# One matmul fewer per tile in k'^T x, and the gate's logits moved into the k product

## The chip, the cores and the metric

The kernel runs on one core of one Trainium2 chip. The metric is the device time of one execution in microseconds (us), as the median of several runs. A core has a matmul engine (PE, with its weight loads shown apart as PEld), a vector engine (DVE), a scalar engine (ACT), GpSimd (POOL) and SP, which here only issues DMAs. Each runs its own queue in order; they wait for each other by semaphores. PE writes its results to PSUM, eight banks of 512 fp32 columns on 128 partitions; DVE and ACT read them from there.

## The reference

With x of 2048 x 576, 32 heads of 18 columns and S = 2048:

```python
g = sigmoid((x * gate_w).sum(-1, keepdims=True))
q, k, v = split(x @ wqkv)                     # 32 heads each
phi = lambda t: where(t > 0, t + 1, exp(t)) + 1e-6
kv  = einsum("bhsd,bhse->bhde", phi(k), v);  z = phi(k).sum over s
o   = (phi(q) @ kv) / (phi(q) . z + 1e-6)
a   = o @ wo
b   = Re(DFT_seq(DFT_hidden(x)))              # by real and imaginary matrices
out = g * a + (1 - g) * b
```

## The kernel before, in words

All matmuls take fp32 numbers as a high part, rounded to the type fp32r, and a low part, what is left. A product is three passes: high x high, high x low, low x high. Making the parts ("a split") costs one ACT copy (`hi_of`, L167) and one DVE subtraction (`lo_of`, L177; `lo_later` queues it until the next `tick()`, L182). D = 576 columns are handled as two halves of HALF = 288. A contraction over 576 rows is five chunks: four of 128 rows with three passes, and a rest of 64, doubled to 128, with two: 14 matmuls (`steps`, L263).

The stages that the change touches, in order:

*The k product* (21.1 to 65.6 us, after a start in which the first four tiles are worked chunk by chunk, L484 to L525). For each of the 16 tiles of 128 rows of x, `k_half(i, h, xs)` (L441) runs 14 matmuls for each half h into a bank, and `k_feature` (L446) calls `feature` (L332): ACT does Relu (L334) on the bank and Exp (L335), DVE combines both (L336) into `acc`. After the second half, `k_split` (L451) splits the feature into `pk`: ACT a copy (L167), DVE L453. It is held back until after the next tile's second half. In a turn of the loop (L551) the program issues: first half; its feature; `split_next` for the tile two ahead; `left_part`, one fifth of the making of a factor for the later Fourier products (two additions, two additions, two ACT copies, a long subtraction, another one); second half; its feature; the split of the tile before.

*k'^T x* (L628). For each chunk c of x's columns, four steps of four tiles run `ps[h] += x_tile^T pk[h]`: two banks `ps[0]`, `ps[1]`, three passes (two in the fifth chunk), two halves, so six (four) matmuls of 288 columns a tile (L637). Steps are numbered 0 to 19 through all chunks; the text calls them so. Around each step x's next tiles are loaded (`xg_load`, SP's queue) into four slots and split (`xg_next`; the tile split in step s is used in step s + 2, its low part is issued after the matmuls of step s + 1). After the second step of a chunk come the kv products of the chunk before (`kv_step`, L619 and L622, 252 and 126 columns), weights of the next stages are loaded and split in between, and at a chunk's end the sum is split into `gt`: two ACT copies of 288 columns (L678) and two DVE subtractions, held back (L679).

*The q product* (`q_tile`, L684) from about 126 us: 14 matmuls for each half and the same `feature`. The weights' second half is 290 columns wide here (QH): its last two columns are `gate_w`, so that column 288 of the bank holds the gate's logit. ACT takes Exp of it (L693), DVE adds one (L695) and takes the reciprocal (L696): the sigmoid, in column i of `gate`, one tile at a time. It is used from `L1124` on and in the Fourier stages behind.

What sets the order: SP's queue is written out by hand for the whole kernel, ACT's and DVE's from `pace()` (L483) to the end, so these three issue in program order. PE's order, until the Fourier stages (L1188), is laid out by a planner at build time: it may put q's matmuls or the kv products between the steps of k'^T x. Waits between engines are put in by the framework from what is read and written.

In the Fourier stage, `Hidden.run` (L906), lines 950 to 957 read one bank, `bx`, with both engines:

```python
if p < NP - 2:
    hi_of(fs(0, 0), bx)
else:
    nc.scalar.activation(t(0), bx, AF.Copy)
add(t(4), bx, t(5))
```

Of the kernel before, what the change touches and what calls it, by code (L numbers as in the profile page):

```python
# [8 lines left out]
F = mybir.dt.float32  # L9
R = mybir.dt.float32r  # L10
# [4 lines left out]
P = 128  # L15
# [56 lines left out]
CONST_AT = Y_AT + 2 * D * 4  # L72
XS = 10 * P * 4
WH, WL = 5 * HALF * 4, 4 * HALF * 4
QH = HALF, HALF + 2


LAY_Q = dict(xs=(-256, 4864, 9984, 43776), hi=(15104, 20864), lo=(26688, 31296))


PRODUCTS = {1: (4, 0), 6: (2, 4), 2: (6, 1), 5: (1, 3), 7: (0, 5), 3: (3, 2), 4: (5, 6)}
# [44 lines left out]
def kernel(  # L126
# [36 lines left out]
    def bank():  # L163
        return psum.tile([P, 512], F, tag="bank", name="bank")
# [34 lines left out]
    def half(h):  # L199
        return slice(h * HALF, (h + 1) * HALF)  # L200
# [80 lines left out]
    class Wide:  # L281
# [6 lines left out]
        def load(self, h, pieces=(KC,), queues=None, also=lambda k: None):  # L288

            n = self.widths[h]  # L290
            cols = slice(h * HALF, h * HALF + n)
            hi = at(self.start + self.lay["hi"][h], [P, 5, n], R, "wd")
            los, c = [], 0
            for k in pieces:
                o = self.start + self.lay["lo"][h] + c * n * 4
                los.append((c, at(o, [P, k, n], R, "wd"), at(o, [P, k, n], F, "wraw")))
                c += k
            rest = at(rest_ring.next(), [P, n], F, "wraw")
            self.got[h] = hi, los, rest
            queues = queues or [nc.sync] * (len(pieces) + 1)  # L300
            for i, (c, _, raw) in enumerate(los):
                also(i)
                queues[i].dma_start(out=raw, in_=self.src[:, c:c + raw.shape[1], cols])
            also(len(los))
            queues[-1].dma_start(out=rest, in_=self.src[:, KC, cols])
# [26 lines left out]
    def feature(dst, ps):  # L332
        e = at(es.next(), [P, HALF], F, "e")
        nc.scalar.activation(e, ps, AF.Relu, scale=-1.0)  # L334
        nc.scalar.activation(e, e, AF.Exp, scale=-1.0)  # L335
        nc.vector.scalar_tensor_tensor(dst, ps, 0.0, e, op0=ALU.max, op1=ALU.add)  # L336
# [97 lines left out]
    K_AT = T_AT + NT * XD  # L434
    pk = [at(T_AT + s * XD, [P, 2, D], R, "pk") for s in range(NT)]
    x_at(LAY_Q)
    wkt = Wide(wk, dict(hi=(0, WH), lo=(2 * WH, 2 * WH + WL)), K_AT)

    done = []

    def k_half(i, h, xs):  # L441
        ps = bank()[:, :HALF]
        run(ps, steps(xs, lambda j: wkt.row(h, j)))
        k_feature(i, h, ps)

    def k_feature(i, h, ps):  # L446
        feature(acc[i][:, half(h)], ps)
        if h == 1:
            pending.append(lambda: k_split(i))

# [4 lines left out]

    C_AT = K_AT + 20736
    first, cuts = [], ((0, 1), (1, 1), (2, 2), (4, 1))
    ab = [slice(k * FT // 2 * P, (k + 1) * FT // 2 * P) for k in range(2)]  # L460

# [20 lines left out]
        load_next()  # L482
    pace()  # L483
    for h in range(2):  # L484
        ps = [bank()[:, :HALF] for _ in range(FT)]
        parts = wkt.split(h, KC)
        for c, (raw, hi, lo) in enumerate(first):
            passes = [(hi, c), (lo, c), (hi, 5 + c)][:3 if c < KC else 2]
            tiles = [range(FT)] * len(passes)
            if h == 0 and c == 0:  # L490
                a, b = ab
                nc.vector.tensor_copy(out=hi[:, a], in_=raw[:, a])
                lo_of(lo[:, a], raw[:, a], hi[:, a])
                next(parts)
                done.append(hi_of(hi[:, b], raw[:, b]))
                lo_of(lo[:, b], raw[:, b], hi[:, b])
                two = range(FT // 2), range(FT // 2, FT)
# [75 lines left out]
    tick()  # L573


    wqt = Wide(wq, LAY_Q, widths=QH)
    wq_splits = (s for h in (1, 0) for s in wqt.split(h, 2, lo_later))
    zacc = at(K_AT + 2 * XD, [P, D], F, "zacc")
    zs = at(K_AT + 3 * XD, [P, 2, D], R, "zs")
# [45 lines left out]
    wvt[0], wv_split = load_pair(wv_ring.next(), wv[:, 0])  # L625
    wo_split = []
    step = 0
    for c in range(5):  # L628
        ps = [bank(), bank()]
        passes = FULL if c < KC else FULL[:2]  # L630
        for q in range(NCU):
            t = xg_split.pop(0)
            for k in range(CU):
                s = q * CU + k
                for n, (a, b) in enumerate(passes):
                    for h in range(2):
                        nc.tensor.matmul(ps[h][:, :HALF], t[:, a, k], pk[s][:, b, half(h)],  # L637
                                         start=(s == 0 and n == 0),
                                         stop=(s == NT - 1 and n == len(passes) - 1))
            tick()  # L640
            xg_load()
            if step == NT - 1:
# [31 lines left out]
                next(wq_splits, None)  # L674
            step += 1
        gt = gts[c] = at(gt_ring.next(), [P, 2, D], R, "gt")
        for h in range(2):
            hi_of(gt[:, 0, half(h)], ps[h][:, :HALF])  # L678
            lo_later(gt[:, 1, half(h)], ps[h][:, :HALF], gt[:, 0, half(h)])  # L679
        left_part()  # L680
    tick()


    def q_tile(i):  # L684
        xs = split.pop(0)
        if i == 0:
            split_next()
        for h in range(2):
            ps = bank()[:, :QH[h]]
            run(ps, steps(xs, lambda j: wqt.row(h, j)))  # L690
            g = gate[:, i:i + 1]
            if h:
                done.append(nc.scalar.activation(g, ps[:, HALF:HALF + 1], AF.Exp, scale=-1.0))  # L693
            feature(acc[i][:, half(h)], ps[:, :HALF])
        nc.vector.tensor_scalar(g, g, 1.0, None, op0=ALU.add)  # L695
        nc.vector.reciprocal(out=g, in_=g)  # L696
        load_next()
        if i:
            split_next()
# [109 lines left out]
        f()  # L809
    kv_step(4)  # L810
    q_tile(1)
    build_kv()
    q_tile(2)
    next(norms)
# [393 lines left out]
def _layouts(inputs):  # L1208
# [27 lines left out]
    def right(w):  # L1236
# [17 lines left out]
        "wk": _rows(wqkv[:, D:2 * D]),  # L1254
        "wq": _rows(np.concatenate([wqkv[:, :D], gw, gw], axis=1)),
        "wv": _rows(wqkv[:, 2 * D:]),
        "wo": inputs["A_wo"],
        "xq": left(x.T),
# [27 lines left out]
```

## Time and profile before

| | |
|---|---|
| median of 3 runs | 732.7 us (732.0 to 732.88) |
| profiled execution, first to last instruction (span) | 730.4 us; its own device time isn't listed |
| PE busy | 724.2 us |
| DVE, ACT busy | 601.0 us, 335.6 us |
| TensorE clock granted | 1.000 |

The profile shows one execution. Each engine's instructions are listed with start, length, and in square brackets the idle time ahead of them with the instruction that ended it. "L637" is line 637 of the kernel. Groups carry a count, busy time, mean length in ns and the idle time before. The chain is followed back from the last instruction to what released each; its rows are start, length, what. Lengths of DVE and ACT rows overlap a little at their ends (the next instruction of the queue may start some 0.08 us before a row's end), so the distance between starts is what a queue pays.

### The profile page before, as it was taken

To read this page: it belongs to the slowest core of one execution; us is meant where nothing else is said; L and a number is where in the kernel's file an instruction comes from. 1 tells how busy PE (TensorE), PEld (TensorE's weight loads), DVE (VectorE), ACT (ScalarE), POOL (GpSimd) and SP (SyncE) were. 2 spreads that over 40 slices of the span, in tenths; PEclk is the share of its full clock that TensorE was granted. 3 is DMA by queue.
4 is the path that set the end of the run, shared out by engine and by line. 5 is a ranking of instruction groups with operands and counts; after the bars stand their busy time and mean duration, and the time that the engine had idled before them with its cause. 6 is when DMAs were issued, how large, how long until landed. Compare 5 with 4: busy or idle time off the path is not lost.

```text
span 730.4 us, 13876 instructions
## 1 busy us (share of the span) xinstructions
PE 724.2 (99%) x5444; PEld 722.4 (99%) x5444; DVE 601.0 (82%) x995; ACT 335.6 (46%) x522; POOL 57.0 (8%) x98
## 2 busy tenths in 40 slices
PE   8999999999999999999999999999999999999998
PEld 8999999999999999999999999999999999999997
DVE  5689866779999948989899989767889988788884
ACT  6898435678644444453344334323535332232231
POOL 1011200051032110000000000000000000000000
PEclk9999999999999999999999999999999999999999
DMA  7286787677477999644475666889964544544440
GB/s 254 84 275 217 265 296 234 226 215 224 155 221 298 362 312 383 211 153 135 165 240 177 228 233 202 296 279 395 374 219 130 171 145 135 156 149 148 152 152 33
DMA packets 54356, 158.82 MB, mean 217 GB/s; under 512 B 6420, under 2 KB 11092, under 8 KB 53268
## 3 DMA queue, kind: packets, MB, share of 16 engines
q1 hardware_dynamic: 45044, 118.90, 48.7%
q0 software_dynamic: 8960, 38.65, 14.6%
q8 instruction: 43, 0.70, 0.4%
q10 hardware_dynamic: 288, 0.39, 0.2%
q14 instruction: 21, 0.17, 0.1%
HBM read 115.05 MB, written 41.39 MB: 214 GB/s over the span
## 4 chain that ended last, share of the span: by engine, by line
PE 96%; DMA 2%; DVE 1%; ACT 0%; issue 0%; SPq 0%; DVEq 0%
PE bank L1058 48%; PE bank L197 23%; PE bank L903 14%; PE bank L637 7%; PE bank L512 2%; PE bank L738 1%; DMA wraw<-in_wk_dram 1%; DMA wf<-wm 1%; DMA craw<-in_xg_dram 1%; PE bank L619 0%; DVE row L1074 0%; ACT xb L167 0%; DVE ys L187 0%; PE bank L622 0%; ACT wd L167 0%
## 5 line engine op out<-in xcount | busy, mean ns | idle before, releaser
L1058 PE MATMUL bank<-fh,c 128*128 128x288 f32 x1792 | 357.5, 295 | 0.0
L1058 PEld LDWEIGHTS bank<-fh,c 128*128 128x128 f32 x1792 | 287.5, 188 | 0.0
L1058 PE MATMUL bank<-fl,c 128*128 128x288 f32 x896 | 264.2, 295 | 0.0
L167 ACT ACTIVATE c<-craw 128x1792 fp32r<-128x1792 f32 (+1 forms) x84 | 121.4, 1447 | 187.1 <-DVE craw L187 166.3
L1058 PEld LDWEIGHTS bank<-fl,c 128*128 128x128 f32 x896 | 168.9, 189 | 0.0
L177 DVE TENSOR_TENSOR c<-craw,c 128x1792 fp32r<-128x1792 f32 (+4 forms) x86 | 142.0, 1653 | 5.9 <-ACT c L167 5.7
L187 DVE TENSOR_TENSOR craw<-craw 128x256 f32<-128x256 f32 (+1 forms) x192 | 98.3, 512 | 25.2 <-DMA craw<-in_ci_dram 12.7
L197 PE MATMUL bank<-wd,xs 128*128 128x288 f32 (+1 forms) x784 | 106.3, 296 | 0.4 <-ACT wd L167 0.4
L197 PEld LDWEIGHTS bank<-wd,xs 128*128 128x128 f32 x784 | 104.7, 188 | 0.6 <-ACT wd L167 0.6
L903 PE MATMUL bank<-wf,xf 128*128 128x288 f32 x588 | 92.1, 297 | 0.2 <-DMA wf<-wm 0.2
L903 PEld LDWEIGHTS bank<-wf,xf 128*128 128x128 f32 x588 | 84.0, 189 | 0.4 <-issue 0.4
L197 PE MATMUL bank<-mw,qs 128*128 128x288 f32 x448 | 63.2, 297 | 0.0
L637 PE MATMUL bank<-pk,c 128*128 128x288 f32 x448 | 61.1, 296 | 0.1
L637 PEld LDWEIGHTS bank<-pk,c 128*128 128x128 f32 x448 | 59.9, 189 | 0.3 <-DVE c L177 0.3
L197 PEld LDWEIGHTS bank<-mw,qs 128*128 128x128 f32 x448 | 59.9, 188 | 0.2 <-DVE qs L177 0.2
L187 DVE TENSOR_TENSOR ys<-bank,ys 128x288 f32<-128x288 f32 x63 | 28.8, 457 | 16.1 <-PE bank L1058 12.4
L336 DVE SCALAR_TENSOR_TENSOR acc<-bank,e 128x288 f32<-128x288 f32 x64 | 28.3, 454 | 15.2 <-ACT e L335 13.7
L177 DVE TENSOR_TENSOR fl<-fl,fh 128x864 fp32r<-128x864 f32 (+1 forms) x32 | 34.6, 1093 | 7.1 <-ACT fh L167 5.8
L167 ACT ACTIVATE fh<-fl 128x864 fp32r<-128x864 f32 (+1 forms) x32 | 29.8, 950 | 16.2 <-DVE fl L187 16.2
L903 PE MATMUL bank<-wf,xr 96*128 96x288 f32 x112 | 33.3, 298 | 0.0
L1123 ACT ACTIVATE acc<-bank,gate 128x288 f32<-128x288 f32 x32 | 16.0, 500 | 35.1 <-PE bank L197 34.8
L187 DVE TENSOR_TENSOR ys<-ys,bank 128x288 f32<-128x288 f32 x47 | 21.2, 450 | 12.6 <-PE bank L1058 12.0
(107 smaller groups left out, 665.9 us busy)
## 6 DMA issues: line engine op xcount, KB each, us to landing
xf<-xm SPq DMA_DIRECT2D x42, 512.0 KB, 7.9
craw<-in_cr_dram SPq DMA_DIRECT2D x32, 512.0 KB, 4.1
craw<-in_ci_dram SPq DMA_DIRECT2D x32, 512.0 KB, 3.5
xraw<-in_xa_dram SPq DMA_DIRECT2D x28, 320.0 KB, 4.3
xm<-xb POOLq DMA_DIRECT2D x8, 1024.0 KB, 5.9
wf<-wm SPq DMA_DIRECT2D x14, 576.0 KB, 5.4
xr<-xr SPq DMA_DIRECT2D x14, 448.0 KB, 8.0
xm<-xb POOLq DMA_DIRECT2D x8, 768.0 KB, 5.9
```

Source lines behind the costliest of these rows:

```text
L167: return nc.scalar.activation(dst, src, AF.Copy, bias=bias)
L177: nc.vector.tensor_tensor(out=dst, in0=src, in1=hi, op=ALU.subtract)
L187: nc.vector.tensor_tensor(out=dst, in0=a, in1=b, op=op)
L197: nc.tensor.matmul(ps, a, b, start=(n == 0), stop=(n == len(pairs) - 1))
L336: nc.vector.scalar_tensor_tensor(dst, ps, 0.0, e, op0=ALU.max, op1=ALU.add)
L512: nc.tensor.matmul(ps[i], x[:, i * P:(i + 1) * P], wkt.row(h, j), start=(c == 0 and n == (0 if h or i < 2 else 2)), stop=(c == KC and n == 1))
L637: nc.tensor.matmul(ps[h][:, :HALF], t[:, a, k], pk[s][:, b, half(h)], start=(s == 0 and n == 0), stop=(s == NT - 1 and n == len(passes) - 1))
L738: nc.tensor.transpose(banks[c // KC][:, (c % KC) * P:(c % KC + 1) * P], a, ident)
L903: nc.tensor.matmul(ps, a, b, start=(start and n == 0), stop=(n == len(ops) - 1), skip_group_check=True)
L1058: nc.tensor.matmul(ps[q], c[x][:, l, k], factors[p](y, f), start=(p == 0 and i == 0), stop=(p == NP - 1 and i == 2))
L1123: done.append(nc.scalar.activation(acc[i][:, half(h)], ps[:, :HALF], AF.Copy, scale=gate[:, i:i + 1]))
```

## The change

Three edits. **k'^T x** takes five matmuls for six in a tile: the bank `ps[0]` now holds 512 columns, x's high part times columns 0 to 255 of pk's high part and, beside them, of its low part, in one instruction; `ps[1]` takes columns 256 to 575, 320 wide. At a chunk's end the two halves of `ps[0]` are added: ACT copies one to SBUF, DVE adds the other to it (`raw`), and both parts are split, the 320-column one at once, the other's low part held back. **PE's order** within this loop is the program's. **The gate's logits** come from the k product: `gate_w` stands behind k's weights for q's, DVE copies column 288 of the second half's bank into `gate` ahead of `feature`, and the sigmoid of all 16 columns is computed once, between q tiles 1 and 2. Layouts move by up to 128 bytes to hold the wider weights.

```diff
-QH = HALF, HALF + 2
+KH = HALF, HALF + 2
+CW = 256, D - 256
...
-    wkt = Wide(wk, dict(hi=(0, WH), lo=(2 * WH, 2 * WH + WL)), K_AT)
+    wkt = Wide(wk, dict(hi=(0, WH), lo=(2 * WH + 64, 2 * WH + WL + 64)), K_AT, KH)
...
     def k_half(i, h, xs):
-        ps = bank()[:, :HALF]
+        ps = bank()[:, :KH[h]]
...
     def k_feature(i, h, ps):
-        feature(acc[i][:, half(h)], ps)
+        if h:
+            nc.vector.tensor_copy(out=gate[:, i:i + 1], in_=ps[:, HALF:HALF + 1])
+        feature(acc[i][:, half(h)], ps[:, :HALF])
...
-    wqt = Wide(wq, LAY_Q, widths=QH)
+    wqt = Wide(wq, LAY_Q)
...
+    in_order = tc.manual_schedule(engines={mybir.EngineType.PE})
+    in_order.__enter__()
     for c in range(5):
-        ps = [bank(), bank()]
-        passes = FULL if c < KC else FULL[:2]
+        ps = [bank(), bank()[:, :CW[1]]]
...
-                for n, (a, b) in enumerate(passes):
-                    for h in range(2):
-                        nc.tensor.matmul(ps[h][:, :HALF], t[:, a, k], pk[s][:, b, half(h)],
-                                         start=(s == 0 and n == 0),
-                                         stop=(s == NT - 1 and n == len(passes) - 1))
+                one, last = dict(start=s == 0, stop=False), s == NT - 1
+                if c < KC:
+                    nc.tensor.matmul(ps[1], t[:, 1, k], pk[s][:, 0, CW[0]:], **one)
+                nc.tensor.matmul(ps[0].rearrange("p (b n) -> p b n", b=2), t[:, 0, k],
+                                 pk[s][:, :, :CW[0]], start=s == 0, stop=last and c == KC)
+                if c < KC:
+                    nc.tensor.matmul(ps[0][:, :CW[0]], t[:, 1, k], pk[s][:, 0, :CW[0]],
+                                     start=False, stop=last)
+                    one["start"] = False
+                nc.tensor.matmul(ps[1], t[:, 0, k], pk[s][:, 0, CW[0]:], **one)
+                nc.tensor.matmul(ps[1], t[:, 0, k], pk[s][:, 1, CW[0]:], start=False, stop=last)
...
-        for h in range(2):
-            hi_of(gt[:, 0, half(h)], ps[h][:, :HALF])
-            lo_later(gt[:, 1, half(h)], ps[h][:, :HALF], gt[:, 0, half(h)])
+        t = at(es.next(), [P, CW[0]], F, "e")
+        raw = at(K_AT + c % 2 * XD + D * 4, [P, CW[0]], F, "graw")
+        nc.scalar.activation(t, ps[0][:, CW[0]:], AF.Copy)
+        add(raw, ps[0][:, :CW[0]], t)
+        hi_of(gt[:, 0, CW[0]:], ps[1])
+        lo_of(gt[:, 1, CW[0]:], ps[1], gt[:, 0, CW[0]:])
+        hi_of(gt[:, 0, :CW[0]], raw)
+        lo_later(gt[:, 1, :CW[0]], raw, gt[:, 0, :CW[0]])
         left_part()
+    in_order.__exit__(None, None, None)
...
-            ps = bank()[:, :QH[h]]
+            ps = bank()[:, :HALF]
             run(ps, steps(xs, lambda j: wqt.row(h, j)))
-            g = gate[:, i:i + 1]
-            if h:
-                done.append(nc.scalar.activation(g, ps[:, HALF:HALF + 1], AF.Exp, scale=-1.0))
-            feature(acc[i][:, half(h)], ps[:, :HALF])
-        nc.vector.tensor_scalar(g, g, 1.0, None, op0=ALU.add)
-        nc.vector.reciprocal(out=g, in_=g)
+            feature(acc[i][:, half(h)], ps)
...
     q_tile(1)
+    done.append(nc.scalar.activation(gate, gate, AF.Exp, scale=-1.0))
+    nc.vector.tensor_scalar(gate, gate, 1.0, None, op0=ALU.add)
+    nc.vector.reciprocal(out=gate, in_=gate)
     build_kv()
```

More of the change, by code (lines that the diff above doesn't have):

```diff
@@ L74 @@
 WH, WL = 5 * HALF * 4, 4 * HALF * 4
-QH = HALF, HALF + 2
-LAY_Q = dict(xs=(-256, 4864, 9984, 43776), hi=(15104, 20864), lo=(26688, 31296))
+KH = HALF, HALF + 2
+CW = 256, D - 256
+LAY_Q = dict(xs=(-256, 4864, 9984, 43776), hi=(15104, 20864), lo=(26624, 31232))
 PRODUCTS = {1: (4, 0), 6: (2, 4), 2: (6, 1), 5: (1, 3), 7: (0, 5), 3: (3, 2), 4: (5, 6)}
@@ L293, in load @@
             los, c = [], 0
+            lo, raw = (at(self.start + self.lay["lo"][h], [P, KC, n], d, name)
+                       for d, name in ((R, "wd"), (F, "wraw")))
             for k in pieces:
-                o = self.start + self.lay["lo"][h] + c * n * 4
-                los.append((c, at(o, [P, k, n], R, "wd"), at(o, [P, k, n], F, "wraw")))
+                los.append((c, lo[:, c:c + k], raw[:, c:c + k]))
                 c += k
@@ L454, in k_split @@
                                        op0=ALU.add, op1=ALU.subtract)
-    C_AT = K_AT + 20736
+    C_AT = K_AT + 20864
     first, cuts = [], ((0, 1), (1, 1), (2, 2), (4, 1))
@@ L484 @@
     for h in range(2):
-        ps = [bank()[:, :HALF] for _ in range(FT)]
+        ps = [bank()[:, :KH[h]] for _ in range(FT)]
         parts = wkt.split(h, KC)
@@ L1253, in _layouts @@
         "xg": twice.reshape(NT, P, 5, P).transpose(2, 1, 0, 3),
-        "wk": _rows(wqkv[:, D:2 * D]),
-        "wq": _rows(np.concatenate([wqkv[:, :D], gw, gw], axis=1)),
+        "wk": _rows(np.concatenate([wqkv[:, D:2 * D], gw, gw], axis=1)),
+        "wq": _rows(wqkv[:, :D]),
         "wv": _rows(wqkv[:, 2 * D:]),
```

## The prediction

> **What bounds the kernel now.** I read the page's head first, then engine use by stage, then the chain that ended last, then each queue around the edits.
>
> ```profile
> span 730.4 us, 13876 instructions
> ...
> PE 724.2 (99%) x5444; PEld 722.4 (99%) x5444; DVE 601.0 (82%) x995; ACT 335.6 (46%) x522; POOL 57.0 (8%) x98
> ```
>
> PE is busy for 724.2 of 730.4 us, so any pause that the change puts into PE lengthens the run by its own length. The change touches two stages, the k product (21.1 to 65.6 us) and k'^T x behind it (to 132). The first in the windows view (columns: stretch and length, then PE, PEld, DVE, ACT and POOL busy, clock, DMA):
>
> ```profile
> 21.10:65.60 44.50, 44.50 (x338) 44.50 (x337) 36.65 (x67) 39.91 (x84) 5.19 (x8) 1.00 0.62 208
> ```
>
> In the k product ACT is busy for 39.9 of 44.5 us and DVE for 36.7: both are nearly full and both run in program order, so there PE's lead over them is what has to be watched.
>
> ```profile
> 21.13 44.55 PE bank L197 x336
> ...
> 99.65 12.85 PE bank L637 x96
> ...
> 185.00 0.55 PE bank L738 x5
> ```
>
> From the chain: a 288-column matmul costs 44.55/336 = 132.6 ns in the k product (3.71 us for a tile's 28), 12.85/96 = 133.9 ns in k'^T x, and a 128-column transpose 0.55/5 = 110 ns.
>
> **Part 1: five instructions for six.** For each of the 16 tiles of a chunk of x columns with all three passes the columns stay 6 x 288 = 1728 = 320 + 512 + 256 + 320 + 320; in the fifth chunk 4 x 288 = 512 + 320 + 320. So 4 x 16 + 16 = 80 instructions go and no column does. What is saved is the part of 133.9 ns that doesn't grow with columns. No 512-column matmul is in this trace; the nearest narrower rows are the kv products, where 252 and 126 columns alternate (weight loads of L619, one pair apart):
>
> ```profile
> 85.04 0.19 PEld L619 LDWEIGHTS bank<-gt,plain 128*126 128x126 f32 x1
> ...
> 85.26 0.19 PEld L619 LDWEIGHTS bank<-gt,plain 128*126 128x126 f32 x1
> ```
>
> A pair takes some 0.225 us. The 126-column one can't be much under the transpose's 110 ns, so 252 columns take 115 to 119, and the line through (252, 117 +-2) and (288, 133.9) has a slope of 0.41 to 0.52 ns per column: the fixed part lies between 0 and 15 ns, the saving between 0 and 80 x 15 = 1.2 us. I take the middle, **-0.7 us**. The 256-column matmul stays above the 110 ns floor, so nothing new is exposed.
>
> The Trainium skill, "TensorE: Matmul & The Clock Gate", section "Back-to-back issue gap", gives some 131 ns as the sustained spacing at 512 columns. Here 288 columns already take 133.9, so the trace speaks against it; by it the edit would save some 80 x 134 ns = 10.7 us, the last rival below.
>
> **Part 2: the logits in the k product.** The matmuls of k's second half get 290 columns for 288, those of q's lose the same two: 224 each, nothing in sum. In q this goes (ns min/median/max):
>
> ```profile
> L693 ACT ACTIVATE gate<-bank x16: 152/171/171, 134.9 to 196.9; 128x1 f32<-128x1 f32 x16
> L695 DVE TENSOR_SCALAR gate<-gate x16: 143/145/147, 137.2 to 198.2; 128x1 f32<-128x1 f32 x16
> L696 DVE RECIPROCAL gate<-gate x16: 162/164/167, 137.4 to 198.4; 128x1 f32<-128x1 f32 x16
> ```
>
> That is 2.7 us of ACT and 4.9 of DVE, all beside PE, which has no gap there: worth nothing. The three operations that replace it lie between q tiles and cost nothing either. In the k product DVE gets 16 copies of one column; by these rows some 0.15 us each, 2.4 us in 44.5 of which DVE has 7.9 to spare. Taken as work, nothing.
>
> But the copy reads the bank that ACT's Relu (L334) reads next. What do two engines on one bank do here? Lines 952 to 955 answer: ACT copies bank `bx` to one tile, DVE adds the same bank to another; neither uses what the other writes.
>
> ```profile
> 268.95 0.41 ACT L167 ACTIVATE fh<-bank 128x288 fp32r<-128x288 f32 x1 [2.50 <-PE bank L903]
> 269.40 0.46 DVE L187 TENSOR_TENSOR fl<-bank,fl 128x288 f32<-128x288 f32 x1 [0.85 <-ACT fh L167]
> L187 DVE TENSOR_TENSOR fl<-bank,fl 128x288 f32<-128x288 f32 x8 | 3.6, 455 | 1.7 <-ACT fh L167 1.4 <-ACT fl L954 0.2
> ```
>
> DVE starts 0.04 us after ACT's read ends, and the group row puts its idle time before all of these additions down to the two ACT reads of that bank (L167, and L954 where line 954 makes it). So reads of one bank by two engines are ordered as the program has them, and the Relu of every second half will wait for DVE's copy, which stands in DVE's queue behind that tile's x split and left part. That is a new wait on the fuller engine. (Here both read the same columns; in the change the columns differ, and this is the rival.)
>
> The Trainium skill, "PSUM — Partial Sum Buffer", section "Terms", counts two engines in one bank as a collision, reads against reads included, whichever columns they read; by that rule different columns don't help. The rows above agree where the columns are the same.
>
> What it costs, first at the start of the stage:
>
> ```profile
> 22.76 0.39 ACT L334 ACTIVATE e<-bank 128x288 f32<-128x288 f32 x1
> 22.89 0.76 DVE L453 SCALAR_TENSOR_TENSOR pk<-acc,pk 128x576 fp32r<-128x576 f32 x1 [0.75 <-ACT pk L167]
> ...
> 27.84 0.82 DVE L177 TENSOR_TENSOR xs<-xraw,xs 128x640 fp32r<-128x640 f32 x1 [0.17 <-ACT xs L167]
> ```
>
> Tile 0's Relu waits for its copy, +0.16. Tile 1's copy follows tile 0's pk split on DVE (22.89 + 0.16 + 0.67), so its Relu starts at about 23.9 for 22.76, +1.1; tile 2's again a pk split later, +2.1; tile 3's copy waits for tile 2's whole feature, +2.8. By then the low part of tile 6's x split (27.84 to 28.66) is 2.8 us late. PE wants it at 28.56 (tiles 4 and 5 from 21.13 at 3.71 us), or 0.26 later for the low half, and now has it 0.2 early: PE pauses **2.6 us**. Then it turns into a ring of two in-order queues. Its pieces now, on ACT and on DVE:
>
> ```profile
> 53.28 0.67 ACT L167 ACTIVATE pk<-acc 128x576 fp32r<-128x576 f32 x1
> 53.86 0.39 ACT L334 ACTIVATE e<-bank 128x288 f32<-128x288 f32 x1
> 54.28 0.45 ACT L335 ACTIVATE e<-e 128x288 f32<-128x288 f32 x1
> 54.63 0.72 ACT L167 ACTIVATE xs<-xraw 128x640 fp32r<-128x640 f32 x1
> ```
>
> ```profile
> 39.23 1.22 DVE L177 TENSOR_TENSOR xb<-xb,xb 128x1024 fp32r<-128x1024 f32 x1
> ...
> 41.40 0.45 DVE L336 SCALAR_TENSOR_TENSOR acc<-bank,e 128x288 f32<-128x288 f32 x1
> 41.77 0.82 DVE L177 TENSOR_TENSOR xs<-xraw,xs 128x640 fp32r<-128x640 f32 x1
> 42.50 0.95 DVE L177 TENSOR_TENSOR xb<-xb,xb 128x768 fp32r<-128x768 f32 x1
> ...
> 45.50 0.76 DVE L187 TENSOR_TENSOR xb<-xb 128x256 f32<-128x256 f32 x2
> ```
>
> From copy to copy, by the starts of neighbouring rows (a row's own length less 0.08 where its neighbour isn't shown): copy 0.18, Relu 0.42, Exp 0.35, pk split 0.58, the next half's Relu 0.42, Exp 0.35, x split on ACT 0.75 until DVE may go on, its low part on DVE 0.73, left part 0.67 to 1.14 (the rows of xb; mean about 0.87), and the next copy: 4.65 us, against PE's 3.71. Today it doesn't close, since ACT's Relu asks only for PE. x splits of tiles 6 to 15 make nine turns: 9 x 0.94 = 8.5 us. With the start, **+11.1**; I bound it by 9 and 13.
>
> k'^T x then begins with its queues late: its third step's tile comes some three turns after tile 15's x split, short of x work at the end, about 13.5 us; PE needs it one k tile and two steps later, 3.71 + 2 x 3.2 = 10.1. **+3.4** (2 to 4.5).
>
> **Part 3: the sum of the two banks, in PE's program order.** At the end of each chunk DVE gets an addition and a split ahead of the x split that PE wants in the second step after.
>
> ```profile
> 107.85 0.95 DVE L177 TENSOR_TENSOR xb<-xb,xb 128x768 fp32r<-128x768 f32 x1
> 108.72 0.69 DVE L177 TENSOR_TENSOR c<-craw,c 128x512 fp32r<-128x512 f32 x1
> ...
> 121.49 0.43 DVE L177 TENSOR_TENSOR c<-craw,c 128x256 fp32r<-128x256 f32 x1 [0.66 <-ACT c L167]
> ```
>
> ```profile
> 122.47 0.69 ACT L167 ACTIVATE gt<-bank 128x288 fp32r<-128x288 f32 x2
> 114.89 0.38 SPq L303 DMA_DIRECT2D wraw<-in_wq_dram  x1
> ```
>
> Third chunk (its last two steps of 24 matmuls begin at 99.65, 3.21 us each, so it ends at 106.07): Copy 0.42, addition 0.42, low part 0.48, left part 1.14, then the x split, 0.69 as in 108.72: 109.2, where PE wants it at 99.65 + 3 x 3.21 = 109.3. Cost 0, cover 0.1 us; I take the first two chunks alike. In the fourth, the Copy takes the place of the gt row, 122.47, on ACT; the low part of step 17's tile (121.49 now) moves to 122.47 + 0.42 + 0.42 + 0.48 = 123.8, 2.3 us later, and PE, which now may not put the kv products ahead of step 17, has only q's first 14 matmuls (1.86 us) to fill in. The left part of 107.85 is also 2 to 3 us later; its store holds SP's wq load (114.89), behind which the last x loads queue. Together 0 to 5 us; I take **+2.5**.
>
> **Sum.** 11.1 + 3.4 + 2.5 - 0.7 = +16.3 us. The profiled span is 730.4; the median of the runs is 732.7, 2.3 above it for what lies around the span, and I add to the median: **749.0**, bounds 9 + 2 + 0 - 1.2 = +9.8 (742) and 13 + 4.5 + 5 = +22.5 (755).
>
> **Rivals.**
> - *Reads of different columns aren't ordered* (for: the rows show equal columns only). The copies then fit DVE's idle time and the k product stays as it is. What is left is Part 3: with its wait, 732.7 + 2.5 - 0.7 = 734.5 (733 to 737). Chance 0.10.
> - *The same, and q's matmuls fill the wait*: 732.7 - 0.7 = 732.0 (731 to 733). Against it: only 14 of them are ready. Chance 0.07.
> - *A matmul's spacing doesn't grow with columns above 288*, and the Relu isn't held: 80 x 133.9 ns = -10.7 us, 722. It decides from the first chunk on, if 512 columns pass in under 150 ns. Against it is the step from 117 to 133.9 ns over 36 columns. This is the faster side. Chance 0.03.
>
> **How the numbers follow.** The forecast has 0.80, nearly all within 740 to 756, so that range holds about 8 in 10. A measurement tells some 0.2% (1.5 us) from no change: slower 0.80 + 0.07 of the first rival; same 0.03 of it and 0.05 of the second; faster 0.02 of the second and 0.03: 0.05.
>
> **What would show it.** Right: ACT's Relu (now L334) in the k product idle for DVE's gate copy, about 1 us a tile; 4.6 us between x splits; PE pauses on xs; the first k'^T x matmul some 11 us later. Wrong: Relu idle only for PE there, and the k product ending by 67 us; then this forecast fails as a whole. For Part 1: 20 matmuls of four tiles in 3.16 us would say 14 ns fixed, in 3.21 none. For Part 3: PE's idle time ahead of step 17.

## The result and the profile after

The changed kernel takes 760.8 us (median of 5, 760.0 to 762.4) beside 732.9 us for the kernel before in the same runs (732.0 to 734.0). The ratio is 1.038, with a 95% interval of 1.0368 to 1.0392. It is 27.9 us slower. The forecast was 749.0 with a range of 740 to 756: the direction was right, the size was too small.

The page after, head and use of the engines:

```profile
span 758.9 us, 13692 instructions
...
PE 735.2 (97%) x5364; PEld 723.4 (95%) x5364; DVE 604.1 (80%) x986; ACT 337.8 (45%) x512; POOL 57.0 (8%) x98
```

The 80 matmuls are gone (5444 to 5364), and DVE, ACT and POOL do the same work as before to 1%. The span grew by 28.5 us all the same, so what is new are pauses and slow stretches of PE. The waits of PE after (columns: what waited for what, total us, times, longest):

```profile
PE bank L198 <- ACT xs L168: 4.8, 8, 2.2
PE bank L643 <- DVE c L178: 4.3, 1, 4.3
PE bank L516 <- DVE wd L178: 3.7, 1, 3.7
PE bank L642 <- DVE c L178: 3.7, 5, 1.5
...
PE bank L198 <- ACT kvb L168: 1.2, 1, 1.2
```

They lie in five places: the k product (xs), step 17 of k'^T x (L643), the start (L516), steps 0, 1, 2, 5 and 13 of k'^T x (L642), and once a product of the q stage (kvb). Of these the start and the last have no term in the forecast. To see what each place costs, take the starts of the same PE rows in both timelines:

| start of | before | after | later by | grown since the row above |
|---|---|---|---|---|
| the loop over tiles (tile 4) | 20.96 | 26.05 | 5.1 | 5.1 |
| tile 15 (before: 20.96 + 11 tiles of 3.71) | 61.8 | 78.35 | 16.6 | 11.5 |
| the kv products of chunk 2 | 112.34 | 134.20 | 21.9 | 5.3 |
| the first transpose | 184.84 | 213.97 | 29.1 | 7.2 |
| the end | 730.4 | 758.9 | 28.5 | -0.6 |

**The k product** goes as forecast. The group of the Relus, and two turns of the timeline (start, length, engine, line; idle time ahead in brackets):

```profile
L336 ACT ACTIVATE e<-bank 128x288 f32<-128x288 f32 x64 | 25.7, 402 | 34.4 <-DVE gate L450 22.6 <-PE bank L198 10.2 <-DVE pz L720 0.8
```

```profile
42.40 0.15 DVE L450 COPY gate<-bank 128x1 f32<-128x1 f32 x1
42.59 0.41 ACT L336 ACTIVATE e<-bank 128x288 f32<-128x288 f32 x1 [1.76 <-DVE gate L450]
...
51.93 0.15 DVE L450 COPY gate<-bank 128x1 f32<-128x1 f32 x1
52.12 0.41 ACT L336 ACTIVATE e<-bank 128x288 f32<-128x288 f32 x1 [2.09 <-DVE gate L450]
```

Relu reads columns 0 to 287 of the bank and the copy column 288, and Relu still starts 0.04 us after the copy's end, having stood 1.76 and 2.09 us for it; 22.6 us in all. So reads of different columns are held in order too, by the waits that the framework puts in. Two turns take 9.53 us. PE's rows show the ring: tile 6 waits 2.16 us, and tile 15 comes nine turns later, (78.35 - 35.82) / 9 = 4.73 us each.

```profile
35.82 4.61 PE L198 MATMUL bank<-wd,xs 128*128 128x288 f32 x21 [2.16 <-ACT xs L168]
...
73.40 4.31 PE L198 MATMUL bank<-wd,xs 128*128 128x288 f32 x28 [0.26 <-ACT xs L168]
78.35 4.32 PE L198 MATMUL bank<-wd,xs 128*128 128x288 f32 x28 [0.64 <-ACT xs L168]
84.17 0.41 PE L642 MATMUL bank<-pk,c 128*128 128x320 f32 x1 [1.50 <-DVE c L178]
```

**The start** holds something that the prediction did not see. DVE, then PE:

```profile
9.77 0.46 DVE L178 TENSOR_TENSOR wd<-wraw,wd 128x288 fp32r<-128x288 f32 x1 [4.58 <-DMA wraw<-in_wk_dram]
```

```profile
10.28 7.88 PE L516 MATMUL bank<-wd,xs 128*128 128x288 f32 x46 [3.71 <-DVE wd L178]
```

The low part of the first piece of k's weights waits for a DMA of k's weights. Before, PE's pause at this place was 0.56 us:

```profile
9.20 11.93 PE L512 MATMUL bank<-wd,xs 128*128 128x288 f32 x88 [0.56 <-ACT wd L167]
```
The reason is an edit of `Wide.load` that is not among the three edits listed ahead of the prediction and of which the prediction says nothing: where each piece of the weights had tensors of its own, one tensor for raw and one for low parts, both at the same memory, now spans all pieces of a half.

```diff
+            lo, raw = (at(self.start + self.lay["lo"][h], [P, KC, n], d, name)
+                       for d, name in ((R, "wd"), (F, "wraw")))
             for k in pieces:
-                o = self.start + self.lay["lo"][h] + c * n * 4
-                los.append((c, at(o, [P, k, n], R, "wd"), at(o, [P, k, n], F, "wraw")))
+                los.append((c, lo[:, c:c + k], raw[:, c:c + k]))
```

A low part is written over its own raw numbers through the other tensor. With one pair of tensors for all pieces, the write into piece 0 is treated as if it touched all of raw, and waits until the other pieces have landed.

**The end of a chunk.** Around step 17, ACT and DVE, then PE:

```profile
144.54 0.63 ACT L168 ACTIVATE c<-craw 128x512 fp32r<-128x512 f32 x1 [0.98 <-DMA craw<-in_xg_dram]
145.25 0.68 ACT L168 ACTIVATE plain<-wraw 128x576 fp32r<-128x576 f32 x1
145.84 0.43 ACT L168 ACTIVATE wd<-wraw 128x288 fp32r<-128x288 f32 x1
146.17 0.36 ACT L690 ACTIVATE e<-bank 128x256 f32<-128x256 f32 x1
```

```profile
146.57 0.42 DVE L188 TENSOR_TENSOR graw<-bank,e 128x256 f32<-128x256 f32 x1 [2.22 <-ACT e L690]
147.56 0.49 DVE L178 TENSOR_TENSOR gt<-bank,gt 128x320 fp32r<-128x320 f32 x1 [0.56 <-ACT gt L168]
147.96 0.41 DVE L178 TENSOR_TENSOR c<-craw,c 128x256 fp32r<-128x256 f32 x1
```

```profile
148.48 0.77 PE L643 MATMUL bank<-pk,c 128*128 128x512 f32 x1 [4.26 <-DVE c L178]
```

Read it backwards. PE waits for the low part of step 17's tile (147.96). DVE had nothing to do for 2.22 us before it, but that low part stands in its queue behind the addition `graw`, the addition waits for ACT's Copy of the bank, and the Copy stands in ACT's queue behind the split of c (step 17's own tile, which had to wait 0.98 us for its load), a split of wv and one of wq. The bank itself had its last matmul by 141.7. So an addition that nobody needs soon carries what holds ACT through two in-order queues to PE. Not all of the 4.26 us is the addition's: ACT was through with step 17's tile only at 145.17, so its low part of 0.41 us could not have been there before 145.6, and PE had finished step 16 at 144.2. Some 1.4 us is the late load. All five additions find DVE idle for the Copy:

```profile
L188 DVE TENSOR_TENSOR graw<-bank,e 128x256 f32<-128x256 f32 x5 | 2.1, 422 | 11.4 <-ACT e L690 11.4
```

That is 11.4 us of idle DVE in sum.

**The clock.** The windows view of PE (stretch, length, busy, clock granted, DMA share, GB/s):

```profile
10.28:14.90 4.62, 4.62 (x23) 0.63 0.79 302
35.80:40.40 4.60, 4.53 (x22) 0.69 0.03 9
148.40:153.00 4.60, 4.52 (x15) 0.50 0.05 18
```

Behind these three pauses PE has a lower clock for some 4.6 us: 0.63 at the start (4.62 x 0.37 = 1.7 us lost), 0.69 behind tile 6's wait, 0.50 behind step 17's (2.3 us lost). The first matmul there has a row of 0.77 us. The clock before was 1.00 throughout. So this pause of 4.26 us costs about 6.5.

The five rows of matmuls of a tile, for part 1 of the forecast:

```profile
140.12 0.39 PE L643 MATMUL bank<-pk,c 128*128 128x512 f32 x1
140.35 0.28 PE L646 MATMUL bank<-pk,c 128*128 128x256 f32 x1
140.47 0.30 PE L649 MATMUL bank<-pk,c 128*128 128x320 f32 x1
140.61 0.31 PE L650 MATMUL bank<-pk,c 128*128 128x320 f32 x1
140.75 0.31 PE L642 MATMUL bank<-pk,c 128*128 128x320 f32 x1
140.90 0.39 PE L643 MATMUL bank<-pk,c 128*128 128x512 f32 x1
```

By the distance of the starts, 512 columns take 0.23 us, 256 take 0.12, 320 take 0.14 to 0.15; this tile takes 140.90 - 140.12 = 0.78 us where six of 133.9 ns took 0.803. Single tiles vary by 0.02 us, so a long stretch tells more: in a later kernel (sum last, own memory for raw) the starts of the first 24 tiles of k'^T x run from 65.69 to 83.88 without a pause, 0.791 us a tile, and before 24 tiles took from 65.51 to 84.69, 0.799 each. That is 8 ns for each instruction that went, 0.7 us for 80.

### The profile page after: what moved, and what is told of

It is laid out like the page before. It is cut to its first block, busy times and chain, and to the rows that moved or that the text cites. A ratio compares the mean times of both kernels' runs of the same rounds, so it can differ in the third digit from the quotient of the medians.

```text
span 758.9 us, 13692 instructions
## 1 busy us (share of the span) xinstructions
PE 735.2 (97%) x5364; PEld 723.4 (95%) x5364; DVE 604.1 (80%) x986; ACT 337.8 (45%) x512; POOL 57.0 (8%) x98
## 4 chain that ended last, share of the span: by engine, by line
PE 81%; DVE 7%; ACT 6%; DMA 4%; issue 2%; SPq 0%; DVEq 0%; ACTq 0%
PE bank L1073 44%; PE bank L198 15%; PE bank L918 14%; PE bank L516 2%; ACT e L337 1%; PE bank L643 1%; ACT e L336 1%; ACT pk L168 1%; PE bank L750 1%; DVE c L178 1%; ACT xs L168 1%; DVE xs L178 1%; DVE xb L178 1%; PE bank L649 1%; PE bank L650 1%
## 5 line engine op out<-in xcount | busy, mean ns | idle before, releaser
L198 PE MATMUL bank<-wd,xs 128*128 128x288 f32 (+1 forms) x784 | 112.7, 301 | 6.6 <-ACT xs L168 4.8
L198 PEld LDWEIGHTS bank<-wd,xs 128*128 128x128 f32 x784 | 106.7, 191 | 11.1 <-ACT xs L168 7.1
L338 DVE SCALAR_TENSOR_TENSOR acc<-bank,e 128x288 f32<-128x288 f32 x64 | 28.4, 455 | 28.1 <-ACT e L337 26.5
L336 ACT ACTIVATE e<-bank 128x288 f32<-128x288 f32 x64 | 25.7, 402 | 34.4 <-DVE gate L450 22.6
L168 ACT ACTIVATE fh<-fl 128x864 fp32r<-128x864 f32 (+1 forms) x32 | 29.8, 950 | 16.1 <-DVE fl L188 16.1
L643 PE MATMUL bank<-pk,c 128*128 128x512 f32 x80 | 32.7, 409 | 4.4 <-DVE c L178 4.3
```

Source lines behind the costliest of these rows:

```text
L168: return nc.scalar.activation(dst, src, AF.Copy, bias=bias)
L198: nc.tensor.matmul(ps, a, b, start=(n == 0), stop=(n == len(pairs) - 1))
L643: nc.tensor.matmul(ps[0].rearrange("p (b n) -> p b n", b=2), t[:, 0, k], pk[s][:, :, :CW[0]], start=s == 0, stop=last and c == KC)
```

## The experiments

All run beside the kernel before, whose median was 733.26 us for the first four below, 733.29 for the next four, 733.42 for the three after and 733.07 for the last. The theory is the reading above: four causes (the copy's place, the shared tensors of the weights' pieces, the chunk's end, the clock after pauses). Its rivals are that the clock or the order of PE does it by itself, or that two of the causes are one.

**The copy behind the feature.** The changed kernel with the two lines of `k_feature` exchanged:

```diff
-        if h:
-            nc.vector.tensor_copy(out=gate[:, i:i + 1], in_=ps[:, HALF:HALF + 1])
         feature(acc[i][:, half(h)], ps[:, :HALF])
+        if h:
+            nc.vector.tensor_copy(out=gate[:, i:i + 1], in_=ps[:, HALF:HALF + 1])
```

> The DVE copy of the gate's column stands behind feature() in the program instead of ahead of it. Theory (the Relu of each second half waits for the copy, and two in-order queues close a ring): the Relu's idle time for the gate copy, 22.6 us, goes; the k product's tiles take 3.71 us again; the run loses some 15 us of its 28, to about 746 us. Rival (16 more DVE operations reading PSUM are themselves what fills the stage, wherever they stand): within 2 us of 760.8. The start (first matmul of the loop over tiles at 26.05 us) stays as it is under both.

Measured: 746.9 us (746.5 to 748.2), ratio 1.0184 (1.0169 to 1.0199), 13.9 us less than the changed kernel. The group of Relus lost its wait for the copy altogether, and PE goes from the loop's start to the end of the k product without a pause:

```profile
L336 ACT ACTIVATE e<-bank 128x288 f32<-128x288 f32 x64 | 25.6, 400 | 16.7 <-PE bank L198 12.5 <-PE bank L516 2.6 <-DVE pz L720 0.8
```

The copies are still there, at the same bank. It was their place ahead of Relu, not their work. The start did not stay quite as it was: in this run's profile the loop over tiles begins at 24.73 for 26.05, so some 1.3 us of the lead may be the start's.

**Own tensors for the pieces.** `Wide.load` as before for the halves of 288 columns (the wider half keeps the new form):

```diff
-            lo, raw = (at(self.start + self.lay["lo"][h], [P, KC, n], d, name)
-                       for d, name in ((R, "wd"), (F, "wraw")))
+            if n != HALF:
+                lo, raw = (at(self.start + self.lay["lo"][h], [P, KC, n], d, name)
+                           for d, name in ((R, "wd"), (F, "wraw")))
             for k in pieces:
-                los.append((c, lo[:, c:c + k], raw[:, c:c + k]))
+                if n == HALF:
+                    o = self.start + self.lay["lo"][h] + c * n * 4
+                    los.append((c, at(o, [P, k, n], R, "wd"), at(o, [P, k, n], F, "wraw")))
+                else:
+                    los.append((c, lo[:, c:c + k], raw[:, c:c + k]))
```

> Only Wide.load is changed: the first half's pieces of k's weights are tensors of their own again, with the same 290-column layout in DRAM. Theory (with one tensor for all pieces the first low split waits for the load of the last piece): DVE's wait of 4.58 us for wraw goes, the loop over tiles starts near 21 us for 26.05, and the run takes about 756 us. Rival (rows of 2312 bytes in DRAM load more slowly): the start stays at 26 us and the time within 1 us of 760.8.

Measured: 758.0 us (757.6 to 758.4), ratio 1.0333 (1.0317 to 1.0348), 2 us above the expectation. DVE's low part of the first piece no longer waits:

```profile
4.76 0.45 DVE L178 TENSOR_TENSOR wd<-wraw,wd 128x288 fp32r<-128x288 f32 x1
```

It starts at 4.76 instead of 9.77, and the loop over tiles begins at 21.09 instead of 26.05. At the first transpose the lead is still 5.5 us (208.49 for 213.97), but the run is only 2.8 us shorter: later, PE now waits 1.0 us for a factor's load and 0.8 for a split of the last stage, 0.3 and 0.2 in the changed kernel. The cause at the start is shown; a part of what it costs is hidden by loads that come when they come.

**Both.**

> Both edits together. Theory that the end-of-chunk block and PE's fixed order cost by themselves: 760.8 - 15 - 5 = 741 us, PE idle some 4 us ahead of step 17 of k'^T x with its clock lowered behind it. Rival (that wait was only the k product's lag passed on): it goes with the lag, and the time is 732 us, just under the kernel before.

Measured: 742.6 us (741.5 to 743.9), ratio 1.0123 (1.0108 to 1.0138). With the copy's wait gone, the pieces are worth 746.9 - 742.6 = 4.3 us; with own pieces, the copy's place is worth 758.0 - 742.6 = 15.4. The rest to the kernel before, 9.4 us, lies behind the k product.

**The five matmuls alone**, put into the kernel before (with the chunk's end and PE's order, without the gate's move and without the edit of `Wide.load`; the diff is the part of the change under `for c in range(5)`).

> The kernel before with k'^T x alone changed (five matmuls, the sum of two banks, PE in program order); the gate is as before. Theory: the same time as e3 within 1 us (about 740 us: the wait ahead of step 17 less 0.9 us for 80 instructions), so that the gate's move itself, done rightly, is worth nothing. Rival (the wait is the k product's lag): 732 us.

Measured: 741.6 us (741.1 to 741.7), ratio 1.0107 (1.009 to 1.0124), 8.3 us over the kernel before: nearly all of the 9.4 us that the two repairs leave. This edit, meant to take work from PE, costs 8.3 us by itself. Its waits of PE in k'^T x and the window behind step 17's wait:

```profile
83.07 0.41 PE L639 MATMUL bank<-pk,c 128*128 128x320 f32 x1 [1.66 <-DVE c L178]
...
129.09 0.76 PE L640 MATMUL bank<-pk,c 128*128 128x512 f32 x1 [4.46 <-DVE c L178]
```

```profile
128.00:134.00 6.00, 4.91 (x17) 0.51 0.21 64
```

```profile
L188 DVE TENSOR_TENSOR graw<-bank,e 128x256 f32<-128x256 f32 x5 | 2.1, 425 | 16.1 <-ACT e L687 16.1
```

1.7 ahead of step 5, 0.5 in two small ones, 4.5 ahead of step 17, 4.91 x 0.49 = 2.4 by the clock, less the dropped instructions' 0.7: 8.4, close to the measured 8.3 (the spans of the two profiles lie 9.3 apart). And the chunk's end is as late without any lag from the k product: the additions stand 16.1 us for the Copy. Ahead of step 5 it is the queues alone:

```profile
79.28 0.69 ACT L168 ACTIVATE plain<-wraw 128x576 fp32r<-128x576 f32 x1 [2.67 <-DMA wraw<-in_wv_dram]
79.87 0.37 ACT L687 ACTIVATE e<-bank 128x256 f32<-128x256 f32 x1
80.27 0.42 DVE L188 TENSOR_TENSOR graw<-bank,e 128x256 f32<-128x256 f32 x1 [2.93 <-ACT e L687]
...
82.33 0.68 DVE L178 TENSOR_TENSOR c<-craw,c 128x512 fp32r<-128x512 f32 x1
```

The chunk's last matmul ended at 78.25, but the Copy comes at 79.87, behind a split of wv that stood 2.67 us for its load. Step 5's low part (82.33), whose tile ACT had split at 75.97, stands behind the addition.

**The gate's move alone**, with the copy where the change has it and own tensors for the pieces (k'^T x as before).

> Only the gate's move: the logits come from the k product with DVE's copy ahead of the feature, the sigmoid is computed once; k'^T x and its PE order are those of the kernel before, and the first half's pieces of k's weights are tensors of their own. Theory: the ring between DVE's copy and ACT's Relu alone, 733.3 + 14 = 747 us, with the loop over tiles 11 us longer and k'^T x waiting some 3 us at its start. Rival (part of the 14 us that moving the copy gave back in the changed kernel came from its end-of-chunk block being hit by the lag): 740 to 743.

Measured: 749.9 us (749.2 to 753.7), ratio 1.0232 (1.0201 to 1.0263): +16.6, 3 more than expected (the profile is of the slowest of the four runs, 753.7). Its timeline has tile 6 waiting 2.12 us and tile 15 at 73.21, nine turns of 4.73 us as in the changed kernel; k'^T x then waits in five places, 2.4 us, and the q product 0.5 us for weights and 1.2 us for `kvb`, a wait that every kernel with the gate's move shows (0.8 to 1.5 us) and the five matmuls alone don't. Where tile 15 starts it is 11.4 us behind the kernel before, at the kv products of chunk 2 (127.58) 15.2: 3.8 us is the late begin of k'^T x without the five matmuls. The five matmuls alone are 2.2 us behind at the same place (114.50).

The three effects add up: 8.3 + 16.6 + (2.8 to 4.3) = 27.7 to 29.2, measured 27.9. So neither edit needs the other to do harm.

**PE's order.** Both repairs, without the two `in_order` lines, so that the planner lays out PE's order as before.

> e3 (copy behind the feature, pieces on their own) without PE's fixed program order in k'^T x: the planner at build time may put kv and q matmuls between the steps again. Theory (the wait ahead of step 17 comes from DVE's and ACT's queues, and there is little that PE could do meanwhile): 742 us, within 2 us of e3's 742.6. Rival (the fixed order itself costs the 9 us): 733 to 735.

Measured: 741.2 us (740.1 to 742.1), ratio 1.0103 (1.0083 to 1.0122), 1.4 us less than with the order held, at the edge of what the spread tells. PE now waits 1.9 us for the addition `graw`, 1.5 and 0.5 for c, 0.5 for gt, with the clock lowered behind (0.73 over 4.6 us). The order is not what costs 8 us: the planner cannot move what DVE and ACT do in program order.

**The sum behind what PE needs.** Both repairs, and the chunk's end in another order: the left part and the held-back low parts (`tick`) come ahead of the addition.

```diff
         nc.scalar.activation(t, ps[0][:, CW[0]:], AF.Copy)
-        add(raw, ps[0][:, :CW[0]], t)
         hi_of(gt[:, 0, CW[0]:], ps[1])
+        left_part()
+        tick()
+        add(raw, ps[0][:, :CW[0]], t)
         lo_of(gt[:, 1, CW[0]:], ps[1], gt[:, 0, CW[0]:])
         hi_of(gt[:, 0, :CW[0]], raw)
         lo_later(gt[:, 1, :CW[0]], raw, gt[:, 0, :CW[0]])
-        left_part()
```

> e3 with DVE's queue at a chunk's end in another order: the left part and the held-back x split come first, the addition of the two banks and its split after them; ACT's Copy and the 320-column high part stay where they were. Theory (the block at a chunk's end holds up the x split that PE needs next): PE's waits of 1.7 us ahead of step 5 and 4.2 ahead of step 17 shrink to under 0.5 and under 2 us, the clock isn't lowered any more (2.4 us), in all 735 to 737 us. Rival (the last x tiles arrive late because SP's wq load is late): the wait of 4.2 us shrinks by less than 1.5 us, 739 to 741.

Measured: 735.6 us (734.0 to 736.5), ratio 1.0027 (1.0015 to 1.0038): 7.0 us of the 9.4 are gone by issuing the same instructions in another order. DVE around the end of chunk 3:

```profile
121.99 0.43 DVE L178 TENSOR_TENSOR c<-craw,c 128x256 fp32r<-128x256 f32 x1 [0.77 <-ACT c L168]
122.74 0.76 DVE L178 TENSOR_TENSOR plain<-wraw,plain 128x576 fp32r<-128x576 f32 x1 [0.32 <-ACT plain L168]
123.53 0.46 DVE L178 TENSOR_TENSOR wd<-wraw,wd 64x288 fp32r<-64x288 f32 x1
124.02 0.42 DVE L188 TENSOR_TENSOR graw<-bank,e 128x256 f32<-128x256 f32 x1
```

Step 17's low part (121.99) now stands ahead of the addition (124.02), and the waits ahead of steps 5 and 17 are gone, the lowered clock with them (the windows of this stage show 1.00). So Part 3's cause is the order of a chunk's end. For step 5 that is the place of the addition in DVE's queue. For step 17 the edit moved two things at once, since the left part now comes earlier too: SP's load of wq waits for the left part's store (5.5 us with both repairs), goes out at 115.32 for 119.29, and with it the load of step 17's tile comes earlier. ACT's split of that tile, with both repairs and here:

```profile
125.33 0.63 ACT L168 ACTIVATE c<-craw 128x512 fp32r<-128x512 f32 x1 [0.93 <-DMA craw<-in_xg_dram]
```

```profile
121.33 0.63 ACT L168 ACTIVATE c<-craw 128x512 fp32r<-128x512 f32 x1 [0.90 <-DMA craw<-in_xg_dram]
```

With both repairs PE had finished step 16 at 125.06, so by these rows some 1.3 of its 4.2 us would have stayed with the addition out of the way. No run separates the two.

**raw in memory of its own.** In the changed kernel `raw` lies in the memory of gt's low half, and ACT's copy of the 320 columns waits for the addition (0.55 us at 147.09). Both repairs, and:

```diff
-        raw = at(K_AT + c % 2 * XD + D * 4, [P, CW[0]], F, "graw")
+        raw = at(Y_AT + 3 * 1184, [P, CW[0]], F, "graw")
```

> e3 with raw, the sum of the two banks, in memory of its own instead of in the place of gt's low part. Theory (two tensors that share memory are waited for as wholes): ACT's high part of 320 columns no longer waits for DVE's addition (0.55 us at each chunk's end), the block is about 1 us shorter, PE's waits ahead of steps 5 and 17 are 0.5 to 1 us shorter each: about 740.5 us. Rival (those waits are real ones, for the bank or the engine): the same waits, 742.6 us.

Measured: 740.0 us (739.3 to 740.4), ratio 1.0086 (1.0068 to 1.0104), 2.6 us less than both repairs. The pauses ahead of steps 5 and 17 are 1.0 and 3.4 us for 1.7 and 4.2, and the clock behind the latter 0.70 for 0.50: 0.7 + 0.8, and 4.91 x (0.50 - 0.30) = 1.0, together 2.5.

**Towards a better kernel.** Three kernels with the sum last: with own memory for raw, the same without the held order, and without the held order but with raw's memory shared.

> The five matmuls with the gate's copy behind feature(), own tensors for the pieces, the sum of the halves behind the left part, and raw in memory of its own (kernel e9_sum_last with the memory of e11_own_raw). Theory (the end of each chunk decides, by the one-engine chain from the stopped bank to the first split): with no wait of TensorE above 1.5 us left between 66 and 190 us, the time is that of before less the 0.9 us of the dropped instructions, plus what is left of the waits, 732 to 734.5 us. Rival (the order of TensorE's program, written out for this stage, costs something by itself): 734.5 to 736.5, no better than e9_sum_last, since it leaves the order as it is.

> The kernel of e12_last_own_raw without the region that holds TensorE to the order in which the program is written. Theory (the end of the chunk decides): within 1.5 us of e12_last_own_raw, 731 to 734.5 us. Rival (the written order costs something by itself): 1.5 to 3 us below e12_last_own_raw.

> The kernel of e9_sum_last (raw still in the memory of gt's low half) without the region of TensorE's order. Theory: 734 to 736 us, as e9_sum_last, since the sum lies behind the splits in program order and the shared memory costs 0.55 us of the low half alone. Rival (the shared memory holds back the high half as well): above 736.

Measured: 735.9 us (ratio 1.0036, 1.0024 to 1.0049), 734.9 (1.0015, 1.0006 to 1.0024) and 734.9 (1.0025, 1.0014 to 1.0035). The first came out above its expectation, at its rival's number (the held order costs something), and no better than the sum last alone. Without the held order the same kernel takes 1.0 us less, the intervals just touching, though still above its expected 731 to 734.5; with raw's memory shared the ratios differ by 0.0002 only. So the held order costs 1.4 us at most, by the two repairs. With the addition out of the way, the shared memory costs nothing that can be told. What is left in the first one's waits:

```profile
PE bank L628 <- DVE gt L178: 1.4, 1, 1.4
PE bank L198 <- ACT kvb L168: 1.3, 1, 1.3
```

A last kernel, built on the first of these three, moved the kv products of chunk 3 one step back, those of chunk 4 ahead of the splits of wo, and the sigmoid behind the sums of the kv blocks:

```diff
-            if q == 1 and c:
+            if q == (2 if c == 4 else 1) and c:
                 kv_step(c - 1)
...
-    for f in wo_split:
-        f()
     kv_step(4)
+    for f in wo_split:
+        f()
     q_tile(1)
+    build_kv()
     done.append(nc.scalar.activation(gate, gate, AF.Exp, scale=-1.0))
     nc.vector.tensor_scalar(gate, gate, 1.0, None, op0=ALU.add)
     nc.vector.reciprocal(out=gate, in_=gate)
-    build_kv()
```

> The kernel of e12_last_own_raw with the kv products of chunk 3 one step later (behind step 18's matmuls for step 17's), those of chunk 4 ahead of the splits of wo, and the gate's sigmoid behind the sums of the kv blocks for ahead of them. The waits of TensorE that e12_last_own_raw still shows in this stage are 1.4 us ahead of the kv products of chunk 3 and 1.3 us ahead of a product of the q tiles that needs a bank of the kv blocks. Theory (the new end of a chunk costs what TensorE waits for it and nothing else): both waits go, and the time is 2 to 3 us below e12_last_own_raw's 735.9, 732.9 to 733.9 us, the same as the kernel before within 0.1%. Rival (the kv products are late for a reason that moves with them, VectorE's backlog, so that the wait comes back one step later): no change, 735 to 737 us, 0.3 to 0.4% above the kernel before.

Measured: 736.8 us (735.2 to 737.6), ratio 1.0044 (1.0029 to 1.0058): the rival's number. The wait for gt went, but PE now got to q's first products 1.6 us ahead of their weights, with a clock of 0.68 behind that and a wait of 0.4, and `kvb` still costs 0.8:

```profile
126.35 0.40 PE L198 MATMUL bank<-wd,xs 128*128 128x288 f32 x1 [1.55 <-ACT wd L168]
```

So no kernel here beats the one before. What makes the `kvb` wait in all kernels with the gate's move stays open: the sigmoid's place alone does not explain it.

## Why the prediction was wrong, point by point

- **Part 1, -0.7: right, with some luck.** A tile takes 0.791 us for 0.799 over long stretches, 8 ns an instruction and 0.7 us for 80; by the prediction's own sign, four tiles' first matmuls lie 3.16 us apart (94.37 to 97.53) where 3.21 were taken before. But the pair of kv products was divided wrongly. The prediction gave both some 0.11 us; in the profile before, the next row starts 0.06 us after a 126-column one (84.81 to 84.87) and 0.16 us after a 252-column one (84.87 to 85.03). That the bound of 0 to 15 ns held is in part luck. The last rival (spacing that doesn't grow) is refuted: 512 columns take 0.23 us, 256 take 0.12.
- **Part 2, the ring, +11.1: right, with 11.5.** The pause of tile 6 is 2.16 us for 2.6, the turn 4.73 us for 4.65. The first two rivals fall with the Relu's 22.6 us, and the run with the copy behind the feature shows that the place of the copy is the whole of it. The trace agrees with the rule of the Trainium skill ("PSUM — Partial Sum Buffer", "Terms") that the prediction weighed: different columns of one bank don't help. What the trace shows is the wait; no run here lets the two reads overlap.
- **Part 2, the late begin of k'^T x, +3.4: right, with 3.8** by the gate's move alone. In the changed kernel the run fell behind by 5.3 between tile 15 and the kv products of chunk 2, and the excess belongs to the first chunks' ends: the five matmuls alone pause 1.7 us ahead of step 5 and are 2.2 behind by then. That was Part 3's share, which the prediction set to zero for "the first two chunks alike".
- **"The three operations that replace it lie between q tiles and cost nothing either": not shown.** Every kernel with the gate's move waits 0.8 to 1.5 us for `kvb` there, and the cause of that wait is open.
- **Part 3, +2.5: the step that failed.** Alone it costs 8.3 us net of the 0.7 that it saves, so 9.0 for 0 to 5. Three things were mis-sized. For the first chunks the prediction counted the Copy, addition and low part from the moment at which the bank stops, "Copy 0.42, addition 0.42, low part 0.48": it costed the instructions, but the Copy first has to get through ACT's queue, ahead of step 5 behind a split that waited 2.67 us for its load. "Cost 0, cover 0.1 us" should have been read as no cover. For the fourth chunk it did put the Copy at its place in ACT's queue and step 17's low part 2.3 us later. With the five matmuls alone that low part came 7.1 us later (128.58 for 121.49): 2.2 by the pauses before it, some 2.1 by the tile's load, 2.3 as counted and 0.5 by the memory that raw shares with gt. PE's wait is 4.3 to 4.5. The late load the prediction had named, but it took the middle of 0 to 5. And it took PE to go on at full speed, where the clock behind that pause cost 2.3 to 2.4 more.
- **Wide.load: a step that was missing.** The edit is part of the change, but stands neither in the diff ahead of the prediction nor in its sum. It is worth 5.1 us at the start of the profile and 2.8 to 4.3 in the time of the whole.

The sum 16.3 lacks 5.1 (start), 0.4 (k product), 1.9 (late begin and the first chunks' ends, 5.3 for 3.4) and 4.7 (7.2 for 2.5, of which the wait for `kvb` is 1.2): 28.4 of the span's 28.5.

## What to carry to other kernels

When an edit puts a small operation into an in-order queue, the cost is the wait of what stands behind it, and that wait is found by walking back through every queue that feeds the operation, DMA included, not by adding lengths. Put a read that nobody needs soon behind what the bottleneck waits for: moving one copy gave back 13.9 us, and moving one addition with its split behind the left part 7.0, at the same work. And when two tensors share memory, check how much of it a write through one is taken to touch: making one tensor of several pieces turned separate waits into one for the last.

## What the runs showed of the hardware

A pause of PE is paid twice, but not always. Behind pauses of 3.4 to 4.6 us (the start, and step 17 where I read it) the clock granted was 0.50 to 0.70 for 4.6 us and more. Behind single pauses of up to 1.7 us it stayed 1.00 (step 5 in the kernels with one there). In between it went either way: two pauses of 1.55 and 0.41 us within 1 us were followed by 0.68 in the last kernel, one of 2.16 us in the changed kernel by 0.69, with own pieces one of 2.11 by 0.63, and with the gate's move alone one of 2.12 by 1.00:

```profile
30.88:35.50 4.62, 4.62 (x23) 0.63 0.03 7
```

```profile
30.64:35.00 4.36, 4.27 (x28) 1.00 0.04 13
```

The first is the kernel with own pieces, the second the one with the gate's move alone, both right behind the pause of tile 6. In the k product this made no difference: both have turns of 4.73 us, since the ring of DVE and ACT, not PE, set the pace there. The Trainium skill ("TensorE: Matmul & The Clock Gate", "What's actually happening") tells of a window of some 3.4 us that runs free and decides on half or full clock. A free window fits one pause that went either way, and 0.63 of 4.62 us is what one window at half clock would make, as an estimate from that page: (3.4 x 0.5 + 1.2) / 4.62 = 0.63. Its condition, a whole window idle, does not fit a lower clock behind 2.1 us.
